# Splitting the FNet matmuls of an FNet + S4D kernel into two row tiles of 64x128

## The chip, the cores and the metric

One core of a Trainium2 chip runs the whole program. The metric is device time in microseconds of one launch. Three runs of the kernel before took 576.3 to 576.42 us, median 576.32 us.

## The reference

Two independent layers whose outputs are laid side by side. A is an FNet mixing layer on x of 2048 x 512: a DFT along the hidden dimension, then one along the sequence, of which the real part is kept. B is an S4D layer on u of 2048 x 512: a kernel K of 2048 taps for each of 512 channels is made from 128 complex exponentials, and convolved with u.

```python
# A
a = einsum("bsd,ed->bse", x, dft_hid_re)
b = einsum("bsd,ed->bse", x, dft_hid_im)
y = einsum("ts,bse->bte", dft_seq_re, a) - einsum("ts,bse->bte", dft_seq_im, b)
# B
dt = exp(log_dt)
A  = -exp(log_A_real) + 1j * A_imag
C  = (C_real + 1j * C_imag) * dt[:, None]
P  = exp((A * dt[:, None])[:, :, None] * arange(L))
K  = 2.0 * einsum("dn,dnl->dl", C, P).real
y  = irfft(rfft(u.T, 2 * L) * rfft(K, 2 * L), 2 * L)[:, :L].T + u * D_skip
# the output is concatenate([A's y, B's y], axis=-1)
```

All arrays are fp32.

## The kernel before

**FNet (class `Fnet`).** The order of the two DFTs is turned round. Eight "s" groups multiply x (stationary) with the sequence matrices: group (t, c) is a block of 512 output positions t of 4 and the real or imaginary matrix c, contracted over 16 k tiles of 128. Then four "p" groups, one for each t, contract the results (stored to DRAM as p and loaded again) with the hidden matrices over 8 k tiles. A group has four accumulators, d = 0 to 3, of 128x512 fp32: a PSUM bank each. All four banks of `a_psum` are in use by one group; the SSM has the other four.

For fp32 accuracy each operand is split into hi and lo, and each (k, d) is three matmuls: hi x hi, hi x lo, lo x hi. Such a group of three is a *step* here. There are 160 k tiles, so 640 steps and 1920 matmuls, with 128x128 weights and 512 moving columns (L382). The moving tile of an s group is one tile of a sequence matrix, used by four steps. Its hi is made by ACT (L233) and its lo by DVE (L238) from a raw tile that SP's queue loads (RAWS = 7 buffers). Only DEPTH = 4 pairs of hi and lo exist: a pair is free when its k tile has gone through d = 3 (`self.plan.put(self.ss)`). In groups 1 to 7 the tiles k = 3, 7, 11 and 15 are "soft": POOL's queue loads hi (L331), ACT makes lo = -hi (L334), and POOL's queue adds the raw tile into lo by DMA (L336). A soft tile takes its buffer early.

In a group the k tiles go one at a time through d = 0 to 3, but the last BATCH = 2 together: d = 0 for both, d = 1 for both, and so on, so that the four accumulators end two steps apart. As soon as one has ended, `evacuate` copies it with ACT (L405; the very last one L400) into one of STAGED = 4 buffers y, and SP's queue stores that (to p, or to the output). The next group's step d = 0 waits for its bank through `self.acc`. The first step of all (`x0_ev`) needs only the first 128 columns of x's first tile, which `load_x0` splits on their own; `load_x1` splits the other 384 columns.

**SSM (class `Ssm`).** DVE builds tables of powers (`tables`, `tables1`, `tables2`: products L627, sums L636) for 16 chunks of 32 channels; PE turns a chunk into taps (L822). For every two chunks a first DFT stage of K follows (L873, then ACT L856 and DVE L858 and L860) and a store to DRAM (xk). The first stage of u (L934) runs early. Then, for each quarter h of the channels and each q of four: load both spectra's pieces, second DFT stage (L1062), copy (ACT L1041), complex product (DVE L1046, L1048, L1079, L1082), first inverse stage (L1089), copy (L1104), store to DRAM (zs). When a quarter's zs is complete, it is loaded again as zl; the inverse's second stage is `inverse` (L1183, h = 0, 1) or `inverse2` (DVE L1152 and L1154, PE L1161, ACT L1166, h = 2, 3), and SP stores it to the output. These matmuls use tiles of the PE array, given by `tile_position`: four of 128x32, eight of 64x32, eight of 32x64, two of 128x64.

**Order.** Every engine's program is written out in advance. `Plan` runs the generators above as processes against a model of the engines with set prices (a step costs 0.683), takes the piece of work that can start first, in case of a tie by urgency, and emits its instructions there. An engine runs its instructions in that order, so a burst of SSM matmuls stands between two given FNet steps. FNet's matmuls have the least urgent rank on PE. `plan.later` holds SSM matmuls that are emitted inside the loop of FNet's steps.

Of the kernel before, what the change touches and what calls it, by code (L numbers as in the profile page):

```python
# [8 lines left out]
F32 = mybir.dt.float32  # L9
# [7 lines left out]
SEQ, DM, NS = 2048, 512, 128  # L17
# [72 lines left out]
class Plan:  # L90
# [14 lines left out]
    def step(self, p, value):  # L105
        self.now = p[0]
        while True:
            try:
                r = p[3].send(value)
            except StopIteration:  # L110
                return
            value = None
            if isinstance(r, Event):
                if r.time is None:
                    r.waiting.append(p)
                    return
                p[0] = max(p[0], r.time)
            elif isinstance(r, Sem):
                if not r.free:
                    r.waiting.append(p)  # L120
                    return
                p[0] = max(p[0], r.free.pop(0))
            else:
                if r[0] != p[5]:
                    p[0] += HOP
                elif r[0] == "dve" and len(r) < 4:
                    p[0] += RESULT
                p[4], p[5] = r, r[0]
                self.ready.append(p)
                return  # L130
            self.now = p[0]
# [72 lines left out]
class Fnet:  # L204
# [154 lines left out]
        self.plan.set(ev)  # L359

    def matmuls(self):
        nc = self.nc
        for g in self.groups:
            still = (self.x, self.x_ev) if g[0] == "s" else (self.w, self.w_ev)
            items, acc = self.items[g], []
            for batch in [[i] for i in items[:-BATCH]] + [items[-BATCH:]]:
                for d in range(4):
                    if batch[0][3] == 0:
                        yield self.acc
                        acc.append(self.psum.tile([128, DM], F32, name="acc"))  # L370
                    for i in batch:
                        k = i[3]
                        yield self.m_ev[i]
                        yield still[1][k] if k or d or g != self.groups[0] else self.x0_ev
                        (shi, slo), (mhi, mlo) = still[0][k], self.m[i]
                        yield "pe", 0.683, None, 6
                        cols = slice(128 * d, 128 * d + 128)
                        three = (shi, mhi), (shi, mlo), (slo, mhi)
                        if still[1][k] is self.x_ev[0] and not d:
                            three = three[::2] + three[1:2]  # L380
                        for n, (l, r) in enumerate(three):
                            nc.tensor.matmul(acc[d], l[:, cols], r, start=k == 0 and n == 0,  # L382
                                             stop=k == len(items) - 1 and n == 2)
                        while self.plan.later:
                            self.plan.later.pop(0)()
                        if d == 3:
                            self.plan.put(self.ss)
                            self.split_ahead -= 1
                            if i[:3] == ("s", 3, 1):
                                self.plan.set(self.x_free[k])  # L390
                    if batch[-1] is items[-1]:
                        self.plan.spawn(self.evacuate(g, d, acc[d]), -1)

    def evacuate(self, g, d, ps):
        yield self.ys
# [803 lines left out]
ISSUE = 1.0  # L1199
SOFTS = {(g, k) for g in range(1, 8) for k in (3, 7, 11, 15)}  # L1200
BATCH = 2


def program(tc, i, o, parts="AB"):
# [71 lines left out]
```

## Time and profile before

| | us |
|---|---|
| median of three runs | 576.32 |
| span of the profiled execution | 575.0 |
| PE busy | 566.1 (98%) |
| PE weight loads busy | 432.1 (75%) |
| DVE busy | 518.0 (90%) |
| ACT busy | 374.5 (65%) |
| POOL busy | 40.2 (7%) |
| DMA | 133.70 MB, mean 233 GB/s |
| granted TensorE clock | 1.000 |

A row of the timeline or of the chain begins with the start in us and the length in us, then the engine, the line, the operation, output <- inputs, the array's tile (rows*columns) and the shapes. "x9" means nine instructions in one row. PEld is the weight load, which overlaps PE. Matmuls are pipelined: a row of 0.39 us overlaps its neighbours, so their pace is read from the starts, not from the lengths. Queues of DMA issues are marked with a q (SPq, POOLq). A row of busy time by stretch has the stretch, its length, and then the busy time of PE, PEld, DVE, ACT and POOL with the number of instructions, the clock, the share of DMA and GB/s.

### The profile page before, as it was taken

How to read it: one execution, taken by the hardware profiler on the slowest of the kernel's cores; microseconds unless marked ns; L12 is line 12 of the kernel's file. 1: busy time of each engine (PE TensorE's matmuls, PEld its weight loads, DVE VectorE, ACT ScalarE, POOL GpSimd, SP SyncE). 2: the span in 40 equal slices, each digit the busy share in tenths (PEclk: the TensorE clock that was granted, in tenths of full speed). 3: DMA queues.
4: the chain of work that ended last, by engine and by line, in shares of the span. 5: the costliest groups of instructions: out<-in, count | busy, mean ns of one | idle time of the engine just before them, and what ended most of it. 6: DMA issues, size and time to landing. Idle time of an engine off the chain costs nothing.

```text
span 575.0 us, 15642 instructions
## 1 busy us (share of the span) xinstructions
PE 566.1 (98%) x6278; PEld 432.1 (75%) x6278; DVE 518.0 (90%) x909; ACT 374.5 (65%) x734; POOL 40.2 (7%) x60
## 2 busy tenths in 40 slices
PE   8999999999999999999999999999999999999997
PEld 6777777788877777778777776777787778776685
DVE  6999999999999999999999999999988999447632
ACT  5789675763778595768668585845688745355623
POOL 0000000010110000100000001001100000000000
PEclk9999999999999999999999999999999999999999
DMA  8999999996559767766896987569998896599994
GB/s 266 316 368 289 284 280 274 281 280 172 138 154 250 206 186 205 201 175 221 213 219 185 233 227 227 132 173 282 269 291 244 228 292 213 127 282 256 257 256 147
DMA packets 147976, 133.70 MB, mean 233 GB/s; under 512 B 47296, under 2 KB 107328, under 8 KB 147648
## 3 DMA queue, kind: packets, MB, share of 16 engines
q1 hardware_dynamic: 138976, 115.54, 66.6%
q0 software_dynamic: 8064, 14.68, 12.7%
q10 hardware_dynamic: 864, 2.49, 1.9%
q8 instruction: 49, 0.80, 0.6%
q14 instruction: 23, 0.19, 0.1%
HBM read 89.95 MB, written 42.73 MB: 231 GB/s over the span
## 4 chain that ended last, share of the span: by engine, by line
PE 72%; DVE 15%; DMA 6%; issue 4%; ACT 1%; SPq 1%; DVEq 0%; ACTq 0%; POOLq 0%
PE acc L382 56%; PE f L1062 5%; PE f L822 4%; DVE prod L627 4%; PE f L1089 3%; DVE t L636 3%; DVE lo L238 3%; DMA raw<-in_sT 2%; PE f L1183 1%; DMA lo<-in_sT 1%; PE f L873 1%; DMA t<-dt_dram 1%; DMA dt_dram<-cs 1%; DMA xt<-in_uG 1%; PE f L1161 1%
## 5 line engine op out<-in xcount | busy, mean ns | idle before, releaser
L382 PE MATMUL acc<-hi,x_hi 128*128 128x512 f32 x640 | 258.0, 403 | 0.1
L382 PE MATMUL acc<-lo,x_hi 128*128 128x512 f32 x640 | 250.0, 391 | 1.0 <-DMA lo<-in_sT 1.0
L382 PE MATMUL acc<-hi,x_lo 128*128 128x512 f32 x640 | 249.5, 390 | 0.0
L627 DVE TENSOR_TENSOR prod<-t,cs 128x1024 f32<-128x1024 f32 (+4 forms) x192 | 163.1, 868 | 1.8 <-ACT t L744 0.6
L382 PEld LDWEIGHTS acc<-hi,x_hi 128*128 128x128 f32 x640 | 120.1, 188 | 49.0 <-issue 23.8
L382 PEld LDWEIGHTS acc<-hi,x_lo 128*128 128x128 f32 x640 | 120.3, 188 | 25.9
L382 PEld LDWEIGHTS acc<-lo,x_hi 128*128 128x128 f32 x640 | 120.2, 188 | 24.5 <-DMA lo<-in_sT 1.4
L233 ACT ACTIVATE hi<-raw 128x512 fp32r<-128x512 f32 x132 | 82.6, 627 | 68.3 <-PE acc L382 54.1
L238 DVE TENSOR_TENSOR lo<-raw,hi 128x512 fp32r<-128x512 f32 x132 | 90.1, 685 | 24.8 <-ACT hi L233 24.8
L636 DVE TENSOR_TENSOR t<-prod 128x512 f32<-128x512 f32 (+4 forms) x192 | 94.1, 511 | 1.0
L643 ACT ACTIVATE square<-t 128x256 f32<-128x256 f32 (+1 forms) x64 | 36.7, 574 | 27.6 <-DVE t L636 25.4
L336 POOL DMA_DIRECT2D lo<-in_sT x28 | 24.3, 867 | 210.5 <-ACT lo L334 74.0
L1041 ACT ACTIVATE uk<-f 128x1024 f32<-128x1024 f32 x32 | 31.1, 1016 | 10.8 <-PE f L1062 7.9
L405 ACT ACTIVATE y<-acc 128x512 f32<-128x512 f32 x47 | 27.8, 594 | 11.7 <-PE acc L382 11.6
L822 PEld LDWEIGHTS f<-t,t 128*32 128x32 f32 x2048 | 29.5, 110 | 6.3 <-issue 4.7
L822 PE MATMUL f<-t,t 128*32 128x64 f32 x2048 | 32.3, 220 | 0.4 <-issue 0.2
L331 POOL DMA_DIRECT2D hi<-in_sT x28 | 15.9, 568 | 190.7 <-PE acc L382 147.7
L1104 ACT ACTIVATE z<-f 128x512 f32<-128x512 f32 x32 | 17.8, 593 | 13.5 <-PE f L1089 12.5
L1046 DVE TENSOR_TENSOR z<-uk 128x512 f32<-128x512 f32 x32 | 21.9, 685 | 4.4 <-ACT uk L1041 2.9
L656 DVE TENSOR_TENSOR t<-square 128x128 f32<-128x128 f32 (+1 forms) x64 | 24.7, 386 | 0.0
L1062 PE MATMUL f<-xt,w 64*32 64x256 f32 x768 | 23.5, 379 | 0.2 <-DMA xt<-xk 0.2
L1048 DVE TENSOR_TENSOR uk<-uk 128x512 f32<-128x512 f32 x32 | 22.1, 690 | 0.9
(104 smaller groups left out, 496.8 us busy)
## 6 DMA issues: line engine op xcount, KB each, us to landing
raw<-in_sT SPq DMA_DIRECT2D x99, 256.0 KB, 5.3
p<-y SPq DMA_DIRECT2D x32, 256.0 KB, 3.9
xk<-xk_sb SPq DMA_DIRECT2D x32, 256.0 KB, 5.2
zs<-z SPq DMA_DIRECT2D x32, 256.0 KB, 4.7
raw<-p SPq DMA_DIRECT2D x32, 256.0 KB, 4.9
hi<-in_sT POOLq DMA_DIRECT2D x28, 256.0 KB, 4.7
lo<-in_sT POOLq DMA_DIRECT2D x28, 256.0 KB, 4.9
xt<-xu SPq DMA_DIRECT2D x24, 256.0 KB, 4.7
```

The lines of the kernel that those rows point to most:

```text
L233: self.nc.scalar.activation(hi, src, AF.Copy)
L238: self.nc.vector.tensor_tensor(lo, src, hi.bitcast(F32), op=OP.subtract)
L336: self.nc.gpsimd.dma_start(lo, src, accum_op=OP.add)
L382: nc.tensor.matmul(acc[d], l[:, cols], r, start=k == 0 and n == 0, stop=k == len(items) - 1 and n == 2)
L405: self.nc.scalar.activation(y, ps, AF.Copy, scale=-1.0 if g[2] == 1 else 1.0)
L627: self.nc.vector.tensor_tensor(p.rearrange("p k d c m -> p k (d c) m"), src.rearrange("p d c l -> p (d c) l")[:, None, :, rows].to_broadca ...
L636: self.nc.vector.tensor_tensor(dst[:, :, :, rows], p[:, 0], p[:, 1, :, ::-1], op=OP.add)
L643: self.nc.scalar.activation(sq, t[:, :, :, m // 2:m], AF.Square)
L656: self.nc.vector.tensor_tensor(t[:, :, 0, m:2 * m:2], box[0][:, :, 0], box[0][:, :, 1], op=OP.subtract)
L822: nc.tensor.matmul(ps[32 * j:32 * j + 32, i], t1[:, d, c], t2[:, d, c], start=c == 0, stop=c == 1, tile_position=(0, 32 * j))
L1041: a.activation(uk[:, r].rearrange("p g c n d -> p g (c n d)"), p, AF.Copy)
L1062: nc.tensor.matmul(got[r][1][32 * xx:32 * xx + 32, g, 256 * c:256 * c + 256], self.w2[rows, 2 * q + r, xx, 32 * c:32 * c + 32], xt[rows].r ...
```

## The change

Each matmul with 128 rows of contraction becomes two with 64 rows, at `tile_position` (0, 0) and (64, 0). The upper half of a step contributes to accumulator d, the lower half to accumulator (d + 2) mod 4, so the two tiles always write different banks; over the four steps of a k tile each accumulator receives both halves. Steps d and d + 2 use the same two banks the other way round, so each step now begins with an instruction that waits, by a semaphore, for the end of the step two before (`told[-2]`). An accumulator is started at d = 0 or 1 of the first k tile and ended at d = 2 or 3 of the last one, so evacuations come in pairs after the last k tile's d = 2 and d = 3. A group's first two k tiles now go together through d, as the last two do (not in the first group). A step is priced at 0.65 instead of 0.683 in the plan, with 12 instructions instead of 6.

```diff
     def matmuls(self):
-        nc = self.nc
+        self.told = []
         for g in self.groups:
             still = (self.x, self.x_ev) if g[0] == "s" else (self.w, self.w_ev)
-            items, acc = self.items[g], []
-            for batch in [[i] for i in items[:-BATCH]] + [items[-BATCH:]]:
+            items, acc = self.items[g], {}
+            head = 1 if g == self.groups[0] else BATCH
+            for batch in [items[:head], *([i] for i in items[head:-BATCH]), items[-BATCH:]]:
                 for d in range(4):
-                    if batch[0][3] == 0:
-                        yield self.acc
-                        acc.append(self.psum.tile([128, DM], F32, name="acc"))
+                    for e in (d, d + 2):
+                        if e not in acc and e < 4:
+                            yield self.acc
+                            acc[e] = self.psum.tile([128, DM], F32, name="acc")
                     for i in batch:
...
-                        yield "pe", 0.683, None, 6
-                        cols = slice(128 * d, 128 * d + 128)
+                        yield "pe", TRIPLE, None, 12
                         three = (shi, mhi), (shi, mlo), (slo, mhi)
...
-                        for n, (l, r) in enumerate(three):
-                            nc.tensor.matmul(acc[d], l[:, cols], r, start=k == 0 and n == 0,
-                                             stop=k == len(items) - 1 and n == 2)
+                        self.step(acc, d, three, k == 0, k == len(items) - 1)
...
-                    if batch[-1] is items[-1]:
-                        self.plan.spawn(self.evacuate(g, d, acc[d]), -1)
+                    if batch[-1] is items[-1] and d >= 2:
+                        for e in (d - 2, d):
+                            self.plan.spawn(self.evacuate(g, e, acc[e]), -1)
+
+    def step(self, acc, d, three, first, last):
+        nc, tc = self.nc, self.tc
+        if len(self.told) > 1:
+            w = nc.tensor.nop(nofuse=True)
+            tc.add_manual_dep(w.ins, self.told[-2],
+                              mybir.DependencyInfo(mybir.DependencyClass.Sync, mybir.DependencyReason.DATA),
+                              reason="two row tiles take turns at a bank")
+        for n, (l, m) in enumerate(three):
+            for r, e in (0, d), (64, (d + 2) % 4):
+                rows = slice(r, r + 64)
+                w = nc.tensor.matmul(acc[e], l[rows, 128 * e:128 * e + 128], m[rows],
+                                     start=first and n == 0 and d < 2,
+                                     stop=last and n == 2 and d >= 2, tile_position=(r, 0))
+        self.told.append(w.ins.name)
...
 BATCH = 2
+TRIPLE = 0.65
```

More of the change, by code (lines that the diff above doesn't have):

```diff
@@ L390, in matmuls @@
                                 self.plan.set(self.x_free[k])
-                    if batch[-1] is items[-1]:
-                        self.plan.spawn(self.evacuate(g, d, acc[d]), -1)
+                    if batch[-1] is items[-1] and d >= 2:
[11 more added lines that the diff above has]
+                rows = slice(r, r + 64)
+                w = nc.tensor.matmul(acc[e], l[rows, 128 * e:128 * e + 128], m[rows], start=first and n == 0 and d < 2,
+                                     stop=last and n == 2 and d >= 2, tile_position=(r, 0))
+        self.told.append(w.ins.name)
     def evacuate(self, g, d, ps):
```

## The prediction

> **What bounds the kernel now.** I read the page's parts 1 and 2 first, then busy time by stretch, then the chain that ended last, then single rows in time. The page: part 1, and of part 2 the slices of DVE.
>
> ```profile
> PE 566.1 (98%) x6278; PEld 432.1 (75%) x6278; DVE 518.0 (90%) x909; ACT 374.5 (65%) x734; POOL 40.2 (7%) x60
> DVE  6999999999999999999999999999988999447632
> ```
>
> PE is busy for 98% of the span, but DVE has eights and nines too, from the second slice to the 34th, which ends at 489 us. Busy time in two stretches (length, then PE, PEld, DVE, ACT, POOL):
>
> ```profile
> 25.00:485.00 460.00, 456.96 (x5081) 349.96 (x5080) 451.90 (x792) 320.92 (x645) 39.98 (x56) 1.00 0.82 231
> 485.00:575.00 90.00, 85.75 (x1106) 63.48 (x1104) 46.34 (x72) 37.79 (x61) 0.00 (x0) 1.00 0.80 220
> ```
>
> Until 485 us DVE works 451.90 of 460 us: a second bound as tight as PE. DVE's rows in time show where the SSM's tables end (L636) and where the last two pieces of its inverse run; beside them the chain's end, and the landing time of the very last store:
>
> ```profile
> 484.83 0.68 DVE L636 TENSOR_TENSOR t<-prod 128x512 f32<-128x512 f32 x1
> ```
>
> ```profile
> 559.08 0.69 DVE L1152 TENSOR_TENSOR zsum<-zl 128x512 f32<-128x512 f32 x1 [0.47 <-DMA zl<-zs]
> ```
>
> ```profile
> 563.80 0.69 DVE L1154 TENSOR_TENSOR zl<-zl 128x512 f32<-128x512 f32 x1
> ```
>
> ```profile
> 494.98 16.55 PE acc L382 x72
> 511.53 1.89 PE f L1062 x64
> 513.42 2.29 PE acc L382 x9
> ...
> 535.92 3.63 PE acc L382 x15
> 539.55 1.14 PE f L1089 x32
> ...
> 565.36 1.12 PE f L1161 x64
> ...
> 567.61 3.19 DMA out_yb<-zl
> 570.80 0.59 ACT y L400
> ```
>
> ```profile
> out_ya<-y ACTq DMA_DIRECT2D x1, 128.0 KB, 2.4
> ```
>
> Two strands end together. FNet's last evacuation starts at 570.80 and its store ends the span at 575.0. The SSM's last store lands at 567.61 + 3.19 = 570.80. From the tables' end (485.5) to there the SSM strand is 85 us of hops: 16.6 us from the kernel's first DFT stage to the first product (through DRAM, 494.98 to 511.53), 28 us of products, 18.4 us through DRAM again (540.69 to 559.08), then DVE, PE, ACT, DMA. FNet matmuls only fill PE meanwhile. So a faster FNet alone moves one of two strands.
>
> **The change part by part.**
>
> *The pace of the matmuls.* Two FNet matmuls in an undisturbed stretch, five intervals apart; their weight load; then two rounds of the eight 64x32 tiles of L1062 in one burst, six rounds apart, and that burst's loads:
>
> ```profile
> 309.81 0.39 PE L382 MATMUL acc<-hi,x_hi 128*128 128x512 f32 x1
> ...
> 310.95 0.39 PE L382 MATMUL acc<-hi,x_lo 128*128 128x512 f32 x1
> ```
>
> ```profile
> L382 PEld LDWEIGHTS acc<-hi,x_hi 128*128 128x128 f32 x640 | 120.1, 188 | 49.0 <-issue 23.8
> L1062 PEld LDWEIGHTS f<-xt,w 64*32 64x32 f32 x768 | 13.9, 106 | 8.4 <-issue 3.6 <-ACT z L1104 0.4 <-ACT x_hi L233 0.4
> ```
>
> ```profile
> 301.87 0.64 PE L1062 MATMUL f<-xt,w 64*32 64x256 f32 x16
> ```
>
> ```profile
> 303.17 0.42 PE L1062 MATMUL f<-xt,w 64*32 64x256 f32 x8
> ```
>
> FNet: (310.95 - 309.81)/5 = 228 ns a matmul. A tile in the burst: (303.17 - 301.87)/6 = 216 ns, with new weights each time. Now 1920 matmuls become 3840 on half the rows, in 1920 pairs that run side by side. A pair costs 228 ns if the excess belongs to 512 moving columns or to 128-column weights, and 216 ns if it belongs to one lone tile that must swap its weights. I take 216: L1062 is the nearest row that has two row tiles. Gain 1920 x 12 ns = 23.0 us on PE; bounds 0 and 23.
>
> The Trainium skill, "TensorE: Matmul & The Clock Gate", Part 3, "The mechanism", says that a weight load overlaps running matmuls only where the row group differs. Strictly read that fails here: a 188 ns load and a matmul of the same rows share one 228 ns interval. Read as the cause of the last 12 ns it gives the same 216, and no gain if it doesn't apply.
>
> *The wait.* Each step of three pairs begins with an instruction that waits for the step two before. Its nearest rows: the last matmul of an accumulator and the evacuation that it releases on an idle ACT, and a semaphore instruction in PE's queue:
>
> ```profile
> 102.26 0.39 PE L382 MATMUL acc<-hi,x_lo 128*128 128x512 f32 x1
> ...
> 102.69 0.60 ACT L405 ACTIVATE y<-acc 128x512 f32<-128x512 f32 x1 [0.20 <-PE acc L382]
> ```
>
> ```profile
> L382 PEldq EVENT_SEMAPHORE  x1: 51/51/51, 3.8 to 3.8; - x1
> ```
>
> The release is seen 0.43 us after the start of that last matmul, so 0.43 - 0.216 = 0.21 us into the step between. Queued behind the waiting instruction are the next step's loads, or an SSM burst; the loads are wanted when the third pair starts, at 0.43 us. The cover is 0.22 us less 0.05: cost 0. With the cover gone it is 0.64 us for every nanosecond late in each of 640 steps (upper end 51 ns, 33 us). Only PE waits there; no DMA queue is behind it.
>
> *The start.* Step 0 now needs columns 256 to 384 of x beside the first 128. Its first matmul before, and the split of the low part of the rest of x:
>
> ```profile
> 4.56 0.80 PE L382 MATMUL acc<-hi,x_hi 128*128 128x512 f32 x1
> ```
>
> ```profile
> 5.15 0.55 DVE L238 TENSOR_TENSOR x_lo<-uk,x_hi 128x384 fp32r<-128x384 f32 x1
> ```
>
> Step 0's second pair needs that part, which is there at 5.70; at 216 ns a pair from 4.56 it would have been due at about 4.8, but the step's own tile is split on the same DVE just before (until about 5.2), and that wait stands in both kernels: +0.7 us, between 0.5 and 0.9.
>
> *The groups' edges.* All four accumulators now end in the last four steps, in pairs, and the next group's second k tile is wanted 0.65 us after its first, not 2.7 us. Around the start of group 3 (157.94): the last matmul before it, the split of its second tile, an evacuation. Then group 7's start and the same split:
>
> ```profile
> 157.71 0.40 PE L382 MATMUL acc<-hi,x_lo 128*128 128x512 f32 x1
> 157.91 0.62 ACT L233 ACTIVATE hi<-raw 128x512 fp32r<-128x512 f32 x1
> 157.94 0.39 PE L382 MATMUL acc<-hi,x_hi 128*128 128x512 f32 x1
> 158.44 0.59 ACT L405 ACTIVATE y<-acc 128x512 f32<-128x512 f32 x1
> 159.99 0.69 DVE L238 TENSOR_TENSOR lo<-raw,hi 128x512 fp32r<-128x512 f32 x1
> ```
>
> ```profile
> 392.39 0.40 PE L382 MATMUL acc<-hi,x_hi 128*128 128x512 f32 x1
> ```
>
> ```profile
> 392.48 0.69 DVE L238 TENSOR_TENSOR lo<-raw,hi 128x512 fp32r<-128x512 f32 x1
> ```
>
> Group 3's second low part is ready at 160.68 and would be wanted at 157.94 + 0.65 + 0.22 = 158.81: 1.9 us late, because its buffer is freed only by the old group's end. Group 7's is ready at 393.17, wanted at 393.26: not late. Two evacuations (2 x 0.59) after 0.43 us of release take 1.6 us, and the steps ahead of the next use cover 1.3 + 0.2: about even, but they stand before the split on ACT. Between 0 and 1.9 I take 1.0 us, midway, at each of 11 edges: +11.0 us on PE (0 to 21). SP's stores p<-y come in pairs; four y buffers cover them, cost 0. POOL's loads into hi and lo start up to 2 us later in a group's head, where two tiles are held for eight steps; that sits in the same 1.0.
>
> *The end.* Evacuations 1 and 3 both follow the last step: +0.6 us (0.59), on FNet's strand.
>
> *The sum.* FNet's strand: 575.0 - 23.0 + 0.7 + 11.0 + 0.6 = 564.3 us. The SSM's strand, if it ends last: 570.80, and as the last store landed at 570.80 + 0.59 + about 2.4 = 573.8, 1.2 us before the end, 572.0. What shifts it: how far FNet is by 485 us:
>
> ```profile
> 0.00:485.00 485.00, 391.21 (x1648) 304.98 (x1649) 1.00 0.82 235
> ```
>
> 1648 x 12 ns less nine edges is 10.8 us, four k tiles (2.73 us each) whose splits DVE does earlier, ahead of the tables: +2.7 us (4 x 0.69). In the tail: the seven FNet blocks between products, 2.29 to 3.63 us, 17.3 in all, shrink by 12/228: -0.9. The last burst starts at 565.36 although DVE is done at 564.49, behind FNet matmuls that would be gone: -0.8. The four tiles no longer loaded in the tail are 1 MB, at 220 GB/s 4.5 us of DMA in it; 35 of the 85 us are stretches with DRAM trips: -1.8. Sum 572.0 + 2.7 - 0.9 - 0.8 - 1.8 = 571.2 us. That is later than 564.3, so it decides. The median of runs, 576.32, is 1.3 above the span: **572.5 us**. A changed order written by the planner (its step price falls to 0.65) can move the tail by one 2.3 us block either way.
>
> **The rivals.**
> - *PE decides after all.* If the tail shrinks with FNet, the end is 564.3 + 1.3 = 565.6, and 554.6 with edges at 0. For it: PE's 98%. Against: DVE's 451.90 of 460.
> - *The pair is no faster.* At 228 ns FNet's strand is 575.0 + 12.3 = 587.3, run 588.6; with half the edge waits filled by SSM bursts 583. For it: no row shows two tiles with 128 columns and 512 moving elements, and FNet alone has the excess.
> - *The wait is exposed*, with pairs at 216. FNet's strand is 564.3 + 0.64 us per ns; it is slower than before by 0.2% from 19 ns a step on, and 51 ns give 597 us, run 598. Against: 0.17 us of cover, in which nothing of PE's is due.
> - *The loads take turns.* Six loads of 188 ns one after another are 1.13 us a step against 0.68 now: up to 860 us. Against: L1062's 64 loads of 106 ns, 6.8 us, pass within a burst of 1.89 us.
>
> For the last one the Trainium skill, "TensorE: Matmul & The Clock Gate", "LDWEIGHTS (loading the stationary operand)", has a rule that speaks against the change: a load's time goes by its columns, not its rows, about columns/1.2 ns, so half the rows save nothing. As an estimate from that page six loads would be 0.64 us a step, no more than the pairs need even in turn, hence no gain and no loss beyond theirs.
>
> **How the numbers follow.** The forecast holds 0.47 (its own range 566 to 577), PE decides 0.18, the pair no faster 0.21, the wait exposed 0.10, loads in turn 0.04. Low: most of PE's case reaches down to 562. High: most of the 583 to 588.6 case, so 588; beyond it stay part of the exposed wait and the loads in turn. Under about 0.2% (1.2 us) a measurement of this kernel can't tell from no change. Faster 0.42 + 0.18 = 0.60, same 0.07, slower 0.33.
>
> **What would show it.** Right: matmul pairs of acc 216 ns apart within a step; gaps on PE of about 1 us at group edges, ended by DVE lo or ACT y; L636 ending at 486 to 489; the chain's end on out_yb, with FNet's last evacuation several us before it. Wrong: pairs at 228; a bubble every third pair (the wait); L636 ending well before 485, or PE idle in the middle because splits are late.

## The result and the profile after

The changed kernel took 620.57 us (median of 4 runs, 617.02 to 622.67) against 576.31 us (575.53 to 576.42) of the kernel before on the same chip: 1.0767 times as long, 95% interval 1.0725 to 1.0809, some 44 us slower. The profiled execution took 618.54 us; its span is 616.8 us.

The page of the changed kernel, of part 1 the engines' line, of part 2 the slices of PE and the granted clock, of part 3 the queue that carries instructions:

```profile
PE 575.8 (93%) x8198; PEld 451.9 (73%) x8198; DVE 521.9 (85%) x909; ACT 372.7 (60%) x734; POOL 40.2 (7%) x60
...
PE   8998999989999999999999989799999989999833
...
PEclk9999999989999999999999999899999999999975
...
q8 instruction: 67, 1.10, 0.7%
```

PE is busy for longer (575.8 against 566.1 us) and yet for a smaller share. The last slices, 8, 3 and 3, are an end in which PE has little left to do, and the granted clock sinks there. Busy time in two stretches, cut where FNet's last matmul ends; first the kernel before (one stretch), then the changed one:

```profile
0.00:570.80 570.80, 566.08 (x6278) 432.08 (x6278) 518.01 (x909) 373.87 (x734) 40.18 (x60) 1.00 0.82 233
```

```profile
0.00:584.60 584.60, 564.86 (x7910) 444.75 (x7910) 512.36 (x895) 365.06 (x720) 40.23 (x60) 0.99 0.77 219
584.60:616.80 32.20, 10.92 (x290) 7.13 (x288) 9.52 (x15) 7.60 (x14) 0.00 (x0) 0.62 0.69 185
```

A span is PE's busy time, its idle time until FNet's end, and its idle time after that. Before: 566.1 + 4.7 + 4.2 = 575.0. After: 575.8 + 19.7 + 21.3 = 616.8. So of 41.8 us, 9.7 are a longer busy time of PE, 15.0 are gaps, and 17.1 are an end without FNet. The pairs of matmuls, which the change was about, gained nothing. Rows of an undisturbed stretch, the first and the last of 27 pairs in a row, and the group of one product's loads (count, busy us, mean ns, then idle time):

```profile
312.62 0.40 PE L406 MATMUL acc<-hi,x_hi 64*128 64x512 f32 x2
...
318.52 0.39 PE L406 MATMUL acc<-hi,x_lo 64*128 64x512 f32 x2
```

```profile
L406 PEld LDWEIGHTS acc<-hi,x_lo 64*128 64x128 f32 x1280 | 135.4, 185 | 22.5 <-issue 0.9 <-DVE x_lo L238 0.5
```

(318.52 - 312.62)/26 = 227 ns a pair, where one whole matmul took 228. The two tiles do run side by side (both in one row "x2"), and their loads too, but the pair has the pace of the single.

The end of the SSM's tables, the row that answers to the 484.83 of before, and the end of the chain that ended last:

```profile
526.40 0.69 DVE L652 TENSOR_TENSOR t<-prod 128x512 f32<-128x512 f32 x1
```

```profile
583.04 1.61 PE acc L406 x12
585.16 0.60 ACT y L416
...
592.71 3.25 DMA out_yb<-zl
596.03 10.98 DMA zl<-zs
...
610.11 1.16 PE f L1177 x28
```

The tables end 41.6 us later (527.1 against 485.5). From there to the end of PE's last matmul of the inverse it is 84.2 us (611.27), against 81.0 before (566.48). So the SSM's strand ends 44.8 us later, and 41.6 of them arise before its tail. It now sets the end of the span; before, FNet's last store did, some 4 us after the SSM's. FNet's last store is issued at 586; what follows is the rest of the inverse alone, 11 us of it one transfer.

Where the gaps are, PE's rows in time around one of them, inside a burst of tap matmuls (the time in brackets is PE's idle time before the row):

```profile
127.31 1.22 PE L838 MATMUL f<-t,t 128*32 128x64 f32 x73
131.18 0.93 PE L838 MATMUL f<-t,t 128*32 128x64 f32 x31 [2.65 <-issue]
132.04 0.79 PE L406 MATMUL acc<-hi,x_hi 64*128 64x512 f32 x2
132.63 0.63 PE L406 MATMUL acc<-lo,x_hi 64*128 64x512 f32 x2
133.06 0.63 PE L406 MATMUL acc<-hi,x_lo 64*128 64x512 f32 x2
```

The burst stops in its middle for 2.65 us while nothing that the profile shows is missing ("issue"). After it the FNet pairs come 430 ns apart, at half pace, for six pairs. Seven gaps of more than 0.3 us between two S4D matmuls sum to 9.7 us in the changed kernel; before there is one of 0.8 us. An eighth, of 3.46 us and also without a visible reason, stands between a burst and the FNet pair behind it (389.36).

### The profile page after: what moved, and what is told of

It is laid out like the page before. It is cut to its first block, busy times and chain, and to the rows that moved or that the text cites. A ratio compares the mean times of both kernels' runs of the same rounds, so it can differ in the third digit from the quotient of the medians.

```text
span 616.8 us, 20118 instructions
## 1 busy us (share of the span) xinstructions
PE 575.8 (93%) x8198; PEld 451.9 (73%) x8198; DVE 521.9 (85%) x909; ACT 372.7 (60%) x734; POOL 40.2 (7%) x60
## 4 chain that ended last, share of the span: by engine, by line
PE 74%; DMA 8%; DVE 6%; ACT 5%; issue 4%; SPq 1%; ACTq 0%; DVEq 0%; POOLq 0%
PE acc L406 59%; PE f L838 5%; PE f L1078 4%; DMA raw<-in_sT 3%; PE f L1105 3%; DMA zl<-zs 2%; DVE prod L643 2%; DMA zs<-z 1%; PE f L889 1%; DMA lo<-in_sT 1%; DVE lo L238 1%; PE f L1199 1%; DVE t L652 1%; PE f L950 1%; DMA xu<-zl 1%
## 5 line engine op out<-in xcount | busy, mean ns | idle before, releaser
L406 PE MATMUL acc<-hi,x_hi 64*128 64x512 f32 x1280 | 274.4, 401 | 5.2 <-issue 3.5
L406 PE MATMUL acc<-lo,x_hi 64*128 64x512 f32 x1280 | 267.2, 390 | 1.3 <-DVE lo L238 1.0
L406 PE MATMUL acc<-hi,x_lo 64*128 64x512 f32 x1280 | 266.6, 389 | 0.3 <-DVE x_lo L238 0.2
L406 PEld LDWEIGHTS acc<-hi,x_hi 64*128 64x128 f32 x1280 | 136.2, 185 | 49.8 <-issue 25.1
L406 PEld LDWEIGHTS acc<-hi,x_lo 64*128 64x128 f32 x1280 | 135.4, 185 | 22.5 <-issue 0.9
L406 PEld LDWEIGHTS acc<-lo,x_hi 64*128 64x128 f32 x1280 | 135.3, 185 | 21.2 <-DVE lo L238 2.4
L838 PE MATMUL f<-t,t 128*32 128x64 f32 x2048 | 33.9, 221 | 7.5 <-issue 7.5
L421 ACT ACTIVATE y<-acc 128x512 f32<-128x512 f32 x47 | 25.5, 597 | 17.9 <-PE acc L406 17.9
L1062 DVE TENSOR_TENSOR z<-uk 128x512 f32<-128x512 f32 x32 | 21.9, 684 | 9.5 <-ACT uk L1057 9.5
L334 ACT ACTIVATE lo<-hi 128x512 fp32r<-128x512 f32 x28 | 17.5, 624 | 9.9 <-DMA hi<-in_sT 9.9
```

Source lines behind the costliest of these rows:

```text
L406: w = nc.tensor.matmul(acc[e], l[rows, 128 * e:128 * e + 128], m[rows], start=first and n == 0 and d < 2, stop=last and n == 2 and d >= 2, ...
L421: self.nc.scalar.activation(y, ps, AF.Copy, scale=-1.0 if g[2] == 1 else 1.0)
L838: nc.tensor.matmul(ps[32 * j:32 * j + 32, i], t1[:, d, c], t2[:, d, c], start=c == 0, stop=c == 1, tile_position=(0, 32 * j))
```

## The experiments

Ratios are to the kernel before on the same chip, with 95% intervals. "Gaps in bursts" are PE's idle times over 0.3 us between two S4D matmuls, "gaps in FNet" those between two FNet matmuls, both added up over the trace's rows until FNet's end.

### The pace: each matmul as two of half the columns

```diff
-    nc.tensor.matmul(acc[d], l[:, cols], r, ...)
+    for h in (slice(0, 256), slice(256, 512)):
+        nc.tensor.matmul(acc[d][:, h], l[:, cols], r[:, h], ...)
```

The step is counted as 12 instructions in the plan. (Diffs here are abridged: `...` stands for what is left out.)

> The kernel before with each FNet matmul made as two of 256 moving columns, with the same 128x128 weights loaded for each; entered with 12 instructions. It prices the excess over the tiles' 216 ns. If it comes with each load of 128 columns: 121 ns a matmul, 241 for the two, if the load's 188 ns set the pace even 376 for the two. If it goes with the moving columns: 114 ns, 228 for the two. The time itself only follows: 575 to 585 us with 228, 600 to 615 us with 241, over 800 us with 376.

601.26 us, ratio 1.0441 (1.0412 to 1.0471). Two of PE's rows, 24 of the smaller matmuls apart, and one group of loads:

```profile
300.09 0.40 PE L383 MATMUL acc<-lo,x_hi 128*128 128x256 f32 x2
...
302.97 0.40 PE L383 MATMUL acc<-lo,x_hi 128*128 128x256 f32 x2
```

```profile
L383 PEld LDWEIGHTS acc<-hi,x_lo 128*128 128x128 f32 x1280 | 199.6, 192 | 1.7 <-issue 1.7
```

(302.97 - 300.09)/24 = 120 ns for 256 columns, 228 for 512. If an interval is a fixed part and a part per column (a straight line through two points, so an estimate), 256 columns are 108 ns and the fixed part is 12 ns. The excess is then paid once per matmul with its 128-column load, and not per moving column. The pair of row tiles, at 227 ns, has no smaller excess than one whole matmul. This kernel pays it twice, and PE is busy for 586.4 us, 20 more than before.

### The wait: next to the step, and far from it

Both kernels put the changed kernel's wait into the kernel before and leave everything else, the order of every engine included:

```diff
+    if len(self.told) > 1:                  # far: > 15
+        w = nc.tensor.nop(nofuse=True)
+        self.tc.add_manual_dep(w.ins, self.told[-2], ...)   # far: told[-16]
...
```

The wait for the step two before:

> The same kernel with the wait, but entered with 6 instructions, so that 640 waits go uncounted as in the changed kernel. Fetch theory: gaps inside bursts come back, 583 to 605 us. Edge and order theories: 575 to 579 us, as with 7.

The same with the wait counted in the plan (7 instructions a step), which also writes another order:

> The kernel before with the wait alone: each step begins with an instruction that waits for the step two before; entered in the plan with 7 instructions instead of 6. Fetch theory: 575 to 579 us, the wait is hidden and counted. Edge and order theories: 575 to 579 us. If the wait itself costs (the prediction's rival): 0.64 us for each ns a step, 590 us and more.

The wait for the step sixteen before:

> The kernel before with the same 640 waits, uncounted as in the run before, in the same order on every engine, but each waits for the step sixteen before, which ended some 10 us earlier. Late-asking theory (a wait on the step two before holds PE's reading of its code within a step of the matmuls, so each next block of code is asked for some 50 instructions later, and bursts run dry): 575 to 577.5 us, no gap over 1 us inside a burst. More-code theory (640 more instructions are enough): 580 to 585 us, the gaps at 112, 137 and 352 us stay.

583.34 us, ratio 1.0123 (1.0086 to 1.016); counted, 587.03 us, 1.0186 (1.0157 to 1.0215); far, 575.44 us, 0.9991 (0.9977 to 1.0004). Neither wait makes a bubble per step: FNet's matmuls keep their 228 ns across a step's end. The near one leaves 5.6 us of gaps in bursts; the same burst of 128 tap matmuls with the near wait, and with the far one:

```profile
350.79 1.65 PE L828 MATMUL f<-t,t 128*32 128x64 f32 x101
355.84 0.64 PE L828 MATMUL f<-t,t 128*32 128x64 f32 x27 [3.41 <-issue]
```

```profile
347.50 1.99 PE L828 MATMUL f<-t,t 128*32 128x64 f32 x128
```

The same instruction, as often, costs 7 to 8 us in the one place (7.1 by the ratio, 8.1 between the medians) and nothing in the other. What differs is how far PE's queue may read ahead. The instruction queue carries one packet for 256 instructions of PE: 49 for the 2 x 6278 of before, 67 for the 2 x 8198 and 638 waits of after. In the trace the k-th packet starts when PE has started 256 k + 217 instructions (median) before and 256 k + 232 with the far wait, but + 263 with the near one and + 280 in the changed kernel. A packet asked for 50 instructions later is no matter among FNet matmuls; in a burst that issues 256 instructions in 2 us it comes too late. In the gap above PE stops at 352.43, a packet starts only then, at 353.38, lands at 354.47, and the burst goes on at 355.84.

That code is what is missing can be read off the traces. Count all that PE starts (matmuls, loads and waits, with the few others in its queue): the burst above goes on after 29 x 256 + 193 of them. So do all gaps over 0.3 us for which the profile names no cause ("issue"): five in this trace, 7.2 us, and eight in the changed kernel, 13.1 us, stand after 256 k + 193 (two of the 13 after + 195), where one packet ends and the next begins. None of the gaps that the profile puts down to an engine does in these two traces. That the near wait is what makes the code come late is shown by the three kernels with one order (before, near, far); how the queue decides to read is not. Nor is the wait the only thing that does it: in the kernels without a wait the median start lies anywhere between 256 k + 209 and 250, and such gaps of up to 2.3 us occur there too (in the kernel before with five pairs of split buffers, below).

### The edges: heads of two, paired evacuations

Together, each alone:

```diff
-    for batch in [[i] for i in items[:-BATCH]] + [items[-BATCH:]]:
+    for batch in [items[:head], *([i] for i in items[head:-BATCH]), items[-BATCH:]]:    # heads
...
-    if batch[-1] is items[-1]:
-        self.plan.spawn(self.evacuate(g, d, acc[d]), -1)
+    if batch[-1] is items[-1] and d >= 2:                                               # pairs
+        for e in (d - 2, d):
+            self.plan.spawn(self.evacuate(g, e, acc[e]), -1)
```

Both:

> The kernel before with the new group edges alone: first two k tiles together from the second group on, evacuations in pairs after d = 2 and d = 3; whole 128x128 matmuls, no wait, old price. Fetch theory: 574 to 580 us. Edge theory: 595 to 615 us, with DVE waiting for ACT's hi at the edges. Order theory: 574 to 580 us.

Heads of two alone:

> The kernel before with only the first two k tiles of a group taken together; evacuations as before. Split theory (the second tile's split is late, because its buffer is freed only by the old group's end): most of the 17.6 us of both edges, 585 to 594 us, with gaps of 1 to 2 us at the second step of groups 1 to 4. Evacuation theory (two accumulators at a time keep ACT and the banks): 575 to 579 us.

Paired evacuations alone:

> The kernel before with only the evacuations in pairs, after d = 2 and d = 3 of the last two k tiles; groups begin one k tile at a time. Split theory: 575 to 580 us. Evacuation theory: 585 to 594 us, PE waiting for ACT's y at the groups' first steps.

Both: 592.82 us, ratio 1.0296 (1.0275 to 1.0316). Heads 586.48, 1.0183 (1.0163 to 1.0203); pairs 583.23, 1.0131 (1.0108 to 1.0154). Each has a cost, where each theory of that pair of runs had given a cost to one of them alone, and they add up: 10.6 + 7.4 against 17.6 us. What PE's FNet matmuls waited for with both (total us, times, longest), and one head on PE, on ACT and on DVE:

```profile
PE acc L384 <- DVE lo L238: 6.7, 7, 1.8
...
PE acc L384 <- ACT y L408: 1.1, 1, 1.1
...
PE acc L384 <- ACT hi L233: 1.0, 1, 1.0
```

```profile
54.39 0.51 PE L384 MATMUL acc<-hi,x_hi 128*128 128x512 f32 x1
56.37 0.50 PE L384 MATMUL acc<-lo,x_hi 128*128 128x512 f32 x1 [1.48 <-DVE lo L238]
```

```profile
53.70 0.63 ACT L233 ACTIVATE hi<-raw 128x512 fp32r<-128x512 f32 x1
```

```profile
54.16 1.22 DVE L630 TENSOR_TENSOR prod<-t,cs 128x1024 f32<-128x1024 f32 x1
55.30 0.42 DVE L653 SCALAR_TENSOR_TENSOR t<-t 128x256 f32<-128x256 f32 x1
55.63 0.69 DVE L238 TENSOR_TENSOR lo<-raw,hi 128x512 fp32r<-128x512 f32 x1
```

These are 8.8 us of stalls over nine waits, about 1 us each. In the head shown, hi is there at 54.33 and the split of lo starts at 55.63, because it stands behind a product of 1.22 us in DVE's queue; the other heads were not followed. The stalls are half of the loss. The order of the engines' programs is another one too (what an order can cost is shown below), and how much of the other half that is stays open.

### The plan's price alone

```diff
-                        yield "pe", 0.683, None, 6
+                        yield "pe", 0.65, None, 6
```

> The kernel before with only the price of a FNet step in the plan changed from 0.683 to 0.65 us: no row tile, no wait, no edge. Theory 'order': 585 to 595 us, since the plan then schedules by a clock that runs 5% fast in FNet's part. Rival 'price is no cause': 573 to 580 us.

602.68 us, ratio 1.0466 (1.0435 to 1.0497): 26.8 us from a number in the plan, with every instruction as it was. Its two stretches, cut at FNet's end:

```profile
0.00:550.70 550.70, 548.54 (x5768) 423.74 (x5768) 504.46 (x881) 360.51 (x713) 40.16 (x60) 1.00 0.79 226
550.70:599.40 48.70, 19.70 (x513) 11.55 (x512) 18.50 (x29) 13.41 (x22) 0.00 (x0) 0.69 0.76 190
```

PE has next to no gaps (2.2 us idle in 550.7), but FNet is through 48.7 us before the end, and 29.0 us of that is idle. Busy time until 160 us, in the kernel before, in this one, and in the changed kernel (PE, PEld, DVE, ACT, POOL):

```profile
0.00:62.00 62.00, 59.99 (x295) 45.14 (x296) 56.34 (x114) 49.62 (x100) 2.32 (x7) 1.00 0.93 310
62.00:160.00 98.00, 97.85 (x971) 76.20 (x970) 96.83 (x167) 62.06 (x129) 10.82 (x15) 1.00 0.84 241
```

```profile
0.00:62.00 62.00, 60.34 (x298) 45.58 (x299) 48.66 (x98) 43.35 (x89) 2.31 (x7) 1.00 0.89 296
62.00:160.00 98.00, 98.00 (x857) 76.99 (x856) 88.52 (x151) 60.13 (x123) 11.35 (x16) 1.00 0.86 253
```

```profile
0.00:62.00 62.00, 58.48 (x500) 47.63 (x508) 47.79 (x96) 43.58 (x90) 2.31 (x7) 1.00 0.89 294
62.00:160.00 98.00, 95.06 (x1163) 75.65 (x1147) 87.54 (x152) 55.68 (x112) 10.79 (x15) 0.98 0.83 241
```

By 160 us DVE has done 16.0 us less than before with the price alone, and 17.8 us less in the changed kernel. The tables' first product sum starts at 61.3 (price) and 61.9 (changed) instead of 45.4 us; it starts at 61 to 64 us in all four kernels with the price of 0.65, and at 45 to 48 in all the others. With the price alone PE is as busy as ever and FNet runs ahead: by 485 us 1710 of its matmuls have started, against 1648 before. These 62, 14 us at 228 ns, are work that FNet then lacks as filler in the tail. In the changed kernel FNet is not ahead by then (3234 halves, 1617 pairs); there its idle end comes from the SSM's delay.

The price as far on the other side (0.716), in the kernel before:

> The kernel before with the price of a FNet step in the plan raised to 0.716 us, as far above 0.683 as the tried 0.65 lay below it; nothing else. Theory 'direction': the price sets how much FNet work is placed ahead of the S4D work; a higher one places less, FNet still runs to the end, and TensorE has no idle tail: 573 to 582 us. Rival 'any other order costs as much': 590 to 605 us.

592.89 us, ratio 1.0315 (1.0282 to 1.0348). "Direction" is right on where FNet ends (4.3 us before the span's end) and wrong on the time: other orders cost as well. Its stretch until FNet's end:

```profile
0.00:587.60 587.60, 572.07 (x6278) 432.79 (x6278) 521.14 (x909) 374.26 (x733) 40.38 (x60) 1.00 0.81 227
```

That is 15.5 us of idle PE instead of 4.7, and for each gap over 0.3 us the profile names an engine or a transfer (the longest 3.8 us, on a copy of ACT). These are not gaps of the code. And the changed kernel with the price put back to 0.683:

> The changed kernel with the price of a step in the plan put back to 0.683 us from 0.65 us, which is what a step takes on the chip (three intervals of 228 ns). Theory 'order': the price of 0.65 makes the plan put too much FNet work, and its copies, ahead of the S4D work, and a right price brings the time down to 600 to 610 us. Rival 'price is no cause': 615 to 626 us, as the changed kernel, since the stalls are in steps that the order does not change.

630.47 us, ratio 1.0894 (1.0811 to 1.0977): no better. The idle end is gone (FNet ends 7 us before the span), and the gaps in bursts have grown from 9.7 to 17.4 us. So the 26.8 us of the price can't be had back by the price alone. The next run counts the wait in the plan of the changed kernel (13 instructions a step):

> The changed kernel with one number altered: a step is entered in the plan with 13 PE instructions (12 and the wait) instead of 12. Fetch theory (the plan keeps its own account of when PE's code arrives, block by block; 640 waits that it doesn't count make the account drift, so SSM bursts are put where the code isn't there yet): the gaps of 1 to 3.7 us inside bursts, 16 us in all, go, DVE idles some 20 us less before the tables end, and the time falls to 585 to 597 us. Edge theory (the new group edges make splits late, and DVE, whose order is fixed, waits with them): 612 to 622 us as before. Order theory (the lower price of a step reorders the early loads and the tables start later): 612 to 622 us.

631.4 us, ratio 1.0946 (1.0885 to 1.1006), 11 us slower than the changed kernel: counting the waits in the plan does not mend it.

### Row tiles without the wait

Each accumulator belongs to one row tile here, so no two tiles meet at a bank:

```diff
-            for r, e in (0, d), (64, (d + 2) % 4):
+            for r, e in (0, d % 2), (64, d % 2 + 2):    # and no wait ahead of the step
...
```

The weights stay those of the changed kernel, so the products of d = 2 and 3 land in the wrong accumulator: these kernels show the time of the matmuls and do not compute the layer.

With the changed kernel's price and count:

> The changed kernel with each accumulator tied to one row tile (accumulators 0 and 1 to rows 0 to 63, accumulators 2 and 3 to rows 64 to 127), so that no two row tiles ever meet at a bank and the wait can be left out. The products of steps d = 2 and 3 land in the wrong accumulator, so that part of the computation is altered; the number, size and order of the matmuls, the loads, the heads of two and the paired evacuations are those of the changed kernel. Theory 'code reading': without the wait PE's reading of its code runs ahead again although there is twice as much of it, no burst of S4D matmuls runs dry in its middle, and the time falls by 8 to 25 us, to 595 to 612 us. Rival 'twice the code by itself': the gaps in the bursts stay with no wait, and the time stays at 615 to 625 us. Under both, a pair of matmuls stays at 227 to 230 ns.

605.68 us, ratio 1.0503 (1.0441 to 1.0566), 14.9 us less than the changed kernel. The gaps in bursts are gone (1.1 us), though the code is the doubled one: packets start at 256 k + 209. Beside the price alone (602.68) the row tiles and edges now cost 3 us. Added up this way, nearly all of the 44 us are the price (26.8) and the wait (14.9). It is one way to add them: the parts depend on each other, as the price put back has shown.

With the old price:

> The row tiles with each accumulator tied to one of them and no wait, as in the run before, now with the price of a step at 0.683 us: edges and row tiles, without the wait and without the new price. As there, the products of steps 2 and 3 land in the wrong accumulator. Theory 'four separate costs': what is left is the edges, 593 us (588 to 598), with TensorE's gaps between FNet matmuls at 8 to 11 us, those inside S4D bursts under 3 us, and FNet running to within 8 us of the end. Rival 'row tiles cost by themselves' (twice the code): 603 to 612 us, with gaps inside bursts.

597.07 us, ratio 1.0376 (1.0346 to 1.0407): near the edges alone, with 7.9 us of gaps in FNet and none in bursts. The changed kernel with that price (630.47) is 33 us slower (30 by the ratios); so the wait costs about twice as much here as with the price of 0.65.

### Two by two, in one order

Four kernels with edges, price 0.683 and count 6 have the same order on every engine: whole matmuls or row tiles, without or with the wait. The edges alone are the first. Whole matmuls with the wait:

> The kernel before with the two things that the change adds beside the row tiles: heads of two k tiles with paired evacuations, and the wait in front of each step for the step two before (counted 6). The FNet matmuls stay whole, 128x128 by 512. Theory 'the parts add up': 17.6 us from the edges and 7.5 us from the wait, so 575.8 + 25 = 601 us (596 to 607), and what is left to the changed kernel's 620.5 (about 19 us) belongs to the row tiles: twice the FNet instructions to be read, and their order. Rival 'the two meet': the edges empty PE's cover and the wait keeps the code from being read ahead, each makes the other worse, and 612 to 625 us comes out without a single row tile; the row tiles would then cost next to nothing.

Row tiles without the wait:

> Edges and row tiles, no wait, the plan's price 0.683 and its count 6 as before: every engine has the order of the kernel with the edges alone (592.8 us), and only each whole FNet matmul has become two half ones. As in the earlier run without the wait, each accumulator is tied to one row tile, and the products of steps 2 and 3 land in the wrong one. Theory 'row tiles are free': pairs at 228 ns, 590 to 596 us, the same as with whole matmuls. Rival 'doubled code costs': bursts run dry without any wait, since twice the code must be read, and 600 to 612 us.

Row tiles with it:

> The changed kernel with the plan's price 0.683 and its count 6 as before: row tiles, wait and edges in the order of the kernel with edges and wait on whole matmuls (607.2 us). Theory 'the wait is worse over doubled code': the wait holds the reading of the code within a step of six matmuls, and a burst has twice as many FNet instructions ahead of it per microsecond, so gaps inside bursts grow past the 12 us of whole matmuls: 612 to 630 us. Rival 'the wait costs the same with either': 603 to 611 us; what the changed kernel loses beyond it is then its order alone.

| | no wait | wait |
|---|---|---|
| whole matmuls | 592.82 us, 1.0296 (1.0275 to 1.0316) | 607.23 us, 1.0514 (1.0466 to 1.0563) |
| row tiles | 597.10 us, 1.0363 (1.0328 to 1.0399) | 620.04 us, 1.0753 (1.0712 to 1.0794) |

What the tap matmuls waited for, by PE's view (total us, times, longest), in the order whole without, whole with, tiles without, tiles with the wait:

```profile
PE f L825 <- issue: 0.9, 1, 0.9
```

```profile
PE f L831 <- issue: 10.6, 4, 3.7
```

```profile
PE f L833 <- issue: 2.9, 2, 1.5
```

```profile
PE f L838 <- issue: 15.0, 7, 3.9
```

The row tiles cost 4 us by themselves, the wait 14.4 us over whole matmuls and 22.9 us over row tiles (12.5 and 22.5 by the ratios, as the runs are from three chips). Over row tiles the kernels without the wait also write other accumulators, so the 22.9 us hold that as well. The last kernel has packets at 256 k + 300, the latest of all. "Row tiles are free" is nearly right, "the wait is worse over doubled code" right. The last kernel has the changed kernel's work in another order and ends at the same time, 620 us: what the price took there as an idle end, this one loses in gaps and in a longer busy time of PE (587.0 us until FNet's end).

### Five pairs of split buffers

```diff
-RAWS, DEPTH, STAGED, AHEAD = 7, 4, 4, 3
+RAWS, DEPTH, STAGED, AHEAD = 5, 5, 4, 3
```

The control, and the edges with it:

> The control of the run with five pairs of split buffers: the kernel before with five pairs of split and five raw buffers and nothing else. Both theories: 571 to 580 us, since TensorE is busy for 566 of the 575 us already; fewer raw buffers could cost some us at the loads.

> Heads of two and paired evacuations on the kernel before, with five pairs of split buffers instead of four (and five raw buffers instead of seven, to make room). Theory 'split buffers freed late': the second tile of a new group can be split while the old group's last two are still read, so the gaps between FNet matmuls fall from 8.5 us to under 4 us, and the time is 576 to 584 us against its control. Rival 'the splits are late for another reason' (DVE and ACT busy elsewhere): gaps and time stay within 4 us of the edges run with four, 589 to 597 us.

597.97 us, ratio 1.0389 (1.037 to 1.0408), and 596.33 us, 1.0361 (1.0334 to 1.0388). The control was not the neutral ground that both theories took it for: with no edges at all it has 18.6 us of idle PE before FNet's end. FNet's matmuls wait there for hi (one wait, 5.0 us) and for the transfers into lo (4.9 us), and tap bursts run dry for 3.2 us although there is no wait in the kernel. So the pair says nothing on how late a head's buffers come free. It costs some 20 us with or without edges; whether by the new order or by the two raw buffers fewer was not separated. No kernel tried beats the one before.

## Why the prediction was wrong

- **The pace, 23.0 us.** The first step that failed. The choice of the L1062 burst as the nearest row was wrong. Its tiles have 32-column weights, and its row says 64x256: the 216 ns are for 256 moving elements, of plain fp32 by the kernel's code, where FNet's 228 ns are for 512 of fp32r. An FNet matmul of 256 takes 120 ns (the run with halves). So 216 and 228 ns were not times of the same work; what sets the burst's 216 ns no run shows. Pairs of 64x128 tiles run at 227 ns, gain 0. The other bound that the prediction gave, "512 moving columns or ... 128-column weights", held, and halving the columns gives the 12 ns to the load or the matmul itself. The rule of the Trainium skill, "TensorE: Matmul & The Clock Gate", Part 3, "The mechanism", that a load overlaps running matmuls only in another row group, has no trace that agrees here: in the run with halves loads of 192 ns pass beside matmuls of the same rows that come every 120 ns, and in the changed kernel, where row groups do differ, nothing is gained. (The same section also lets a load into a background weight buffer be pulled ahead, which would fit; no run here tells.)
- **"The pair is no faster"** was the rival with 0.21, and its FNet strand, 587.3 us, nearly came (the last evacuation ends at 585.8, its store follows): the part on FNet's strand was right. The run it gave, 588.6, did not, since the SSM's strand ended last.
- **The wait, cost 0.** Right that no step waits: pairs across a step's end are 228 ns apart, as within one. Wrong in "Only PE waits there; no DMA queue is behind it". PE's own code comes by a DMA queue, and the wait holds its reading back. It costs 7 to 8 us over the kernel before and 14.9 in the changed one. The rival "the wait is exposed" had the right part and the wrong mechanism. "The loads take turns" did not come: loads of 185 ns run side by side (188 ns with all 128 rows).
- **The order, "one 2.3 us block either way".** The largest miss. The price of 0.65 stood in the diff and was given one sentence; alone it costs 26.8 us, though putting it back in the changed kernel returns nothing. With the pace unchanged it also is the wrong price: three intervals of 228 ns are 0.684.
- **The groups' edges, +11.0 us (0 to 21).** About right as stalls (8.8 us with whole matmuls, 1 us each). In the changed kernel FNet's matmuls waited 2.7 us on y and lo, since its bursts stood elsewhere. The time lost with whole matmuls was larger, 17.6 us; how much of it is order stays open.
- **The start, +0.7.** PE waits 0.20 us for the rest of x_lo. **The end, +0.6:** it came (0.49 us between the starts of the last two evacuations), on a strand that did not decide.
- **The sum.** "The SSM's strand decides" was right and 44 us off: it was to lose 2.7 us before the tables' end and lost 41.6. "PE idle in the middle" was on the list of what would show the prediction wrong, for late splits; the code was not on it.
- **The bound.** The prediction set aside PE's 98% for DVE's 451.90 of 460 us. Both hold at once: with 9 us of idle PE in 575, and DVE as full until 485 us, there was little room for a stall or for another order. How the rest of the 41.6 us before the tables' end divides between price, wait and edges depends on the order in which they are taken out, and stays open.

## What to carry to other kernels

Where an engine is 98% busy, read a change first as a risk to its 2%. Price what each new instruction does to the engine's reading ahead, and treat each number in the plan as an edit of its own, with a run of it alone. Put a wait as far from what it waits for as the hazard allows; sixteen steps away it was free, two steps away it was not. And take the nearest row for a price by what it shares with the new instruction (here the weight columns, the moving elements and the type), not by the feature that is new.

## What the runs showed of the hardware

- A pair of 64x128 row tiles with 512 moving elements keeps the interval of one 128x128 matmul, 227 against 228 ns; loads of 185 ns run side by side.
- FNet matmuls with new weights each take 228 ns for 512 columns and 120 for 256; by a straight line through the two, 12 ns do not depend on the columns. Loads of 192 ns of the same rows hide under the 120 ns intervals.
- PE's code comes in packets of 256 instructions, and PE can run dry where one packet ends: all 13 gaps of the changed kernel and of the near wait that the profile calls "issue" stand there. A semaphore wait for work two steps back, which never shows as a stall, puts the reading of the code off by some 50 instructions, and bursts of small matmuls 2 us long run dry for up to 3.9 us; the same wait sixteen steps back does not.
- After the gap of 2.65 us matmuls run at half pace (430 against 228 ns); the granted clock is 0.50 from 131.40 to 134.81 us. The Trainium skill, "TensorE: Matmul & The Clock Gate", Part 1, "What's actually happening", puts the fall to half rate after an idle window of about 3.4 us; here a shorter gap came before such a fall, while after the near wait's gap of 3.41 us the clock stayed at 1.00. So the length of the gap alone does not decide it.
- In the changed kernel PE is busy for 15.5 us under a granted clock of 0.50: 6.8 after gaps (131.40 to 134.81 and 390.81 to 394.22) and 8.7 in the end (588.78 to 592.19, and from 595.61). If work takes twice as long there, as the pairs above did, that makes about 7.7 of PE's 9.7 us more of busy time, an estimate.
